# Head quads instead of head pairs in a chunk-selected attention kernel with an MLP behind it

## The chip, the core and the metric

The kernel runs on one core of a Trainium2 chip. The metric is device time in microseconds (us), from the first to the last work of one execution; lower is better. The engines are TensorE (PE; its weight loads are listed apart as PEld), VectorE (DVE), ScalarE (ACT), GpSimd (POOL) and SyncE (SP), which here only issues DMA. Each works through its own instructions in order and waits on semaphores for the others.

## What is computed

Attention over 4 batches and 8 heads of 768 tokens with head dimension 64, each query attending to at most 6 chunks of 32 keys, and a gated MLP on the result. Cut to what matters:

```python
k_min, k_max = k_chunks.min(axis=3), k_chunks.max(axis=3)            # 24 chunks of 32 keys
ub = sum(maximum(q * k_min, q * k_max), axis=-1)                     # bound of each query on each chunk
ub = where(causal, ub, -1e9)
top_chunks = argsort(ub)[..., -6:]
scores = where(chunk of key in top_chunks & (pos_q >= pos_k), q @ k.T / 8, -1e9)
attn = softmax(scores) @ v                                           # x: [4*768, 512]
h = x @ w_in                                                         # 512 -> 2048
out = (h * clip(h + 3, 0, 6) / 6) @ w_out                            # 2048 -> 512, fp32
```

## The kernel before, in words

Heads are worked on in 16 pairs (`i`, four to a batch); the MLP takes half batches of 384 tokens (`g`, 0 to 7). The whole program is a list of short tokens, `ORDER`, written out by hand or by a planner; each token calls one function, and each engine gets its instructions in the order of the list. Nothing is reordered later.

Queries below 192 need no selection, so bounds and masks cover the last 576 (`NQ`). For a pair the tokens are:

- `LK`, `LQ`, `LV` load halves of K, Q and V (pairs 0 to 3), `lk`, `lq`, `lv` whole ones (pairs 4 to 15). For pairs 4 to 15 `load_turned` (L230) reads K and Q in rows of 32 numbers (128 bytes), four DMAs for a pair's K and four for its Q, and `kd`, `qd` (L246, L249) turn them on VectorE in 32x32 blocks; pairs 0 to 3 are turned by TensorE (`KT`, `QT`, L379).
- `kb`, `kp`, `qb` make bf16 copies on ACT or POOL, `mx`, `mn` (L344) reduce K over chunks, `rp` makes relu(q).
- `ud` (L472) computes the bounds of two pairs as f32 matmuls in tiles of 64 rows and 32 columns; `us`, `tr`, `tm`, `se`, `tb` add the causal bias, turn, take the 8 largest of 24, compare with the sixth and turn back, on DVE. `mr` (L499) moves half of the mask rows to the partitions where the mask pass needs them.
- `S.i.u.c` is a unit of scores of a pair in PSUM buffer `c` (a, b or c, two banks each, one head to a bank). There are six units (`UNITS`). The two heads lie in two tiles of 64 rows (L549). For pairs 0 to 9 a second matmul (L554) adds -8192 where a chunk is not chosen. `ex` (L560) takes the exponential on ACT, `af` (L567) the causal triangle on POOL.
- Pairs 10 to 15 (`PRODUCT`) have no mask pass on TensorE. Their masks go to HBM (`sm`, L522: four DMAs a pair), come back spread over 128 partitions (`ml`, L527), are made causal (`am`, L534) and are multiplied onto the exponentials by VectorE (`mu`, L541).
- `A` and `B` (L583) are the products with V for the lower and upper 384 queries, `na`, `nb` the division; `X`/`xe` or the DMA transposes `xt` turn the result for the MLP.

For a half batch, `H.g.f` (L627) is 8 hidden matmuls into one of the buffers a, b, c; `hu` (L635, ACT) and `gt` (L638, DVE) make the gate; `O.g.t.n` (L665) is 4 of the 16 output matmuls of a 128-row tile, in the one-bank buffers x, y as a rule; `ot` (L672) unloads it on ACT and `sa` stores it from the ACT queue (L679). The last tile named by an `st` token is projected and stored in two halves.

At the start, POOL builds the identity (`PRI`), then the bias and mask patterns (`PRP`, L279 to L289, `EG`, L297); DVE clears the buffer `WARM` (`PRD`, L269) and the mask pattern EM (`PRL`, L294); five warm-up matmuls (`Z`, L301) read `WARM`.

SP's loads, mask stores and transposes share eight semaphore lanes: a DMA on a lane waits until the one before it on that lane has landed, and everything behind it on the queue waits too.

Of the kernel before, what the change touches and what calls it, by code (L numbers as in the profile page):

```python
# [9 lines left out]
A = mybir.AluOpType  # L10
# [24 lines left out]
LQ.0.0.0 PRD AQ.0.0.1 AK.0.0.1 LQ.0.1.1 LK.0.0.0 LQ.0.1.0 LK.0.1.0 LK.0.1.1 LQ.2.0.0 LQ.2.0.1 LK.1.0.0 Z.b.5  # L35
AK.1.0.1 PRI QT.0.0.y RP.0.0 PRL RN.0.0 KT.0.0.x LK.2.0.1 AQ.1.0.1 LK.2.0.0 MX.0.0 QT.0.1.b RA.0.1 RP.0.1 QB.0.1
KT.0.1.a PRP EG.3 EG.2 LK.1.1.1 LQ.1.0.0 LK.3.0.0 EG.0 QB.0.0 LQ.2.1.1 LK.1.1.0 MN.0.0 UH.0.0.c QT.2.0.b MN.0.1
MX.0.1 RP.2.0 QB.2.0 KT.1.0.y UB.0.0 LQ.2.1.0 MN.1.0 LQ.1.1.0 KB.0.0 LQ.1.1.1 UH.0.1.c MX.1.0 RN.2.0 LK.3.0.1 KB.0.1
UB.0.1 KT.2.0.x MX.2.0 TH.0.0.a QT.1.0.b QB.1.0 EG.1 KB.1.0 TH.0.1.c MN.2.0 T8.0.0 LQ.3.0.0 LQ.3.0.1 RN.1.0 KB.2.0
KT.1.1.y LK.2.1.1 RP.1.0 QT.2.1.x LK.3.1.0 LK.2.1.0 KB.1.1 T8.0.1 AV.1.0.1 RA.2.1 RP.2.1 QB.2.1 UH.1.0.b SE.0.0  # L40
UH.2.0.a SE.0.1 MN.1.1 UB.1.0 QT.1.1.c RA.1.1 QB.1.1 RP.1.1 TH.1.0.b MX.1.1 LK.3.1.1 UB.2.0 LQ.3.1.0 T8.1.0 QT.3.0.x
RN.3.0 LV.1.0.0 VC.1.0 KT.3.0.y MN.3.0 SE.1.0 TH.2.0.a UH.1.1.c MX.3.0 QB.3.0 UB.1.1 LH.0.0.b LV.0.1.0 AV.0.0.1
MT.0.0 RP.3.0 KT.2.1.x T8.2.0 KB.3.0 LH.0.1.c MT.0.1 SE.2.0 KB.2.1 MX.2.1 TH.1.1.y MN.2.1 S.0.1.b ex.0.1 S.0.0.c
S.0.4.a LQ.3.1.1 ex.0.0 ex.0.4 LV.0.0.0 wl.0 af.0.1 af.0.0 VC.0.0 UH.3.0.b LV.0.1.1 T8.1.1 UB.3.0 LV.2.0.0 KT.3.1.x
MN.3.1 MX.3.1 QT.3.1.c RP.3.1 RA.3.1 QB.3.1 UH.2.1.b SE.1.1 KB.3.1 UB.2.1 S.0.3.a ex.0.3 A.0.y LH.1.0.c MT.1.0
af.0.3 LH.2.0.b MT.2.0 TH.2.1.x LV.1.1.1 S.0.5.c ex.0.5 wc.0 VC.0.1 af.0.5 LV.3.0.1 na.0 LV.1.1.0 S.1.0.b ex.1.0
# [687 lines left out]
```

## Time and profile before

| what | value |
|---|---|
| median of 3 runs | 284.36 us |
| the runs | 282.49, 285.15, 284.36 us |
| span of the profiled execution | 279.9 us |
| its own time beside the span | not on the page; the runs lie 2.6 to 5.2 us above the span |
| PE / PEld / DVE / ACT / POOL busy | 256.5 / 150.8 / 199.9 / 176.8 / 84.8 us |
| DMA packets | 137745, of which 122736 under 512 bytes |
| bytes moved | 46.79 MB; HBM read 36.31, written 8.06 |
| mean granted TensorE clock | 0.985 |

The span runs from the first to the last instruction. Busy time of an engine is the time in which at least one of its instructions is under way; TensorE's matmuls overlap, so a busy PE may still start fewer matmuls than it could. Issuing a DMA is not counted as busy, though it holds the engine that issues it.

### The profile page before, as it was taken

Reading aid. Unit: us, or ns where it says so; the run is one execution under the profiler, and the core shown is the slowest. Engines: PE = TensorE matmul, PEld = TensorE weight load, DVE = VectorE, ACT = ScalarE, POOL = GpSimd, SP = SyncE. Lnnn points to the kernel's source line nnn. Section 1 sums busy time; section 2 is a strip of 40 time slices with the busy share of each in tenths; the row PEclk is TensorE's granted clock in tenths of the full one; section 3 lists DMA queues with packets and bytes.
Section 4 is the critical chain, followed back from the end, with each engine's and each line's share of the span. In section 5 each row is a group of like instructions: output and inputs, shape, how many; then the busy total and the mean of one; then the engine's idle time right before and its main releaser. Section 6 shows DMA issues by size and latency. Waiting matters only on the chain.

```text
span 279.9 us, 6893 instructions
## 1 busy us (share of the span) xinstructions
PE 256.5 (92%) x2639; PEld 150.8 (54%) x2661; DVE 199.9 (71%) x490; ACT 176.8 (63%) x245; POOL 84.8 (30%) x159
## 2 busy tenths in 40 slices
PE   6799998899998999976998976899999999999994
PEld 2467775555445476633545543574455557655543
DVE  3697996997777799939967796575988567735500
ACT  2689994457476899734577659267975678234331
POOL 8216857343315656002006322204222411000000
PEclk9999999999999999997999999799999999999998
DMA  8987897997997899887859869585969641130033
GB/s 165 201 196 207 130 346 122 328 264 190 210 189 165 167 175 171 150 169 135 214 147 227 173 180 193 127 241 86 223 169 291 199 99 38 41 93 0 37 115 112
DMA packets 137745, 46.79 MB, mean 167 GB/s; under 512 B 122736, under 2 KB 128368, under 8 KB 137712
## 3 DMA queue, kind: packets, MB, share of 16 engines
q1 hardware_dynamic: 132000, 39.73, 64.6%
q10 hardware_dynamic: 5712, 6.62, 6.8%
q8 instruction: 21, 0.34, 0.5%
q14 instruction: 12, 0.10, 0.1%
HBM read 36.31 MB, written 8.06 MB: 158 GB/s over the span
## 4 chain that ended last, share of the span: by engine, by line
PE 61%; DMA 10%; SPq 8%; issue 6%; DVE 5%; POOL 4%; ACT 4%; ACTq 0%; DVEq 0%; POOLq 0%
PE PBb L627 8%; PE PSy L665 8%; PE PBa L627 8%; PE PBc L627 8%; PE PSx L665 7%; SPq L230 6%; DMA QS<-in_q_dram 3%; DMA out_dram<-OT 3%; PE PSx L583 3%; PE PBa L665 2%; PE PBb L665 2%; POOL PT L567 2%; PE PSy L583 2%; SPq L522 2%; ACT PT L560 2%
## 5 line engine op out<-in xcount | busy, mean ns | idle before, releaser
L627 PEld LDWEIGHTS <-WIN 128*128 128x128 bf16 x512 | 49.5, 99 | 35.3 <-issue 1.8
L665 PEld LDWEIGHTS <-GT 128*128 128x128 bf16 x368 | 34.6, 99 | 40.6 <-issue 3.7
L560 ACT ACTIVATE PT<-PBa 128x1024 bf16<-128x1024 f32 (+2 forms) x33 | 30.9, 937 | 16.1 <-PE PBa L549 11.4
L665 PE MATMUL PSy<-WOUT,GT 128*128 128x512 bf16 x149 | 38.3, 385 | 1.1 <-issue 0.7
L567 POOL TENSOR_SCALAR_AFFINE_SELECT PT<-PT 128x256 bf16<-128x256 bf16 x72 | 30.5, 444 | 24.5 <-ACT PT L560 18.3
L627 PE MATMUL PBb<-XT,WIN 128*128 128x384 bf16 x176 | 33.4, 335 | 1.1 <-POOL WIN L262 1.1
L635 ACT ACTIVATE U<-PBb 128x768 bf16<-128x768 f32 x22 | 17.9, 813 | 20.9 <-PE PBb L627 20.9
L560 ACT ACTIVATE PT<-PBb 128x1024 bf16<-128x1024 f32 (+2 forms) x32 | 29.1, 909 | 3.2 <-PE PBb L554 2.2
L665 PE MATMUL PSx<-WOUT,GT 128*128 128x512 bf16 x119 | 30.1, 382 | 0.7 <-issue 0.3
L627 PE MATMUL PBa<-XT,WIN 128*128 128x384 bf16 x168 | 30.7, 326 | 0.0
L627 PE MATMUL PBc<-XT,WIN 128*128 128x384 bf16 x168 | 30.7, 326 | 0.0
L583 PEld LDWEIGHTS <-PT 128*128 128x128 bf16 x672 | 24.1, 98 | 11.7 <-POOL PT L567 4.5
L560 ACT ACTIVATE PT<-PBc 128x1024 bf16<-128x1024 f32 (+2 forms) x31 | 28.7, 927 | 2.2 <-PE PBc L549 1.6
L635 ACT ACTIVATE U<-PBc 128x768 bf16<-128x768 f32 x21 | 17.0, 811 | 19.3 <-PE PBc L627 19.3
L638 DVE SCALAR_TENSOR_TENSOR GT<-U,PBc 128x768 bf16<-128x768 bf16 x21 | 19.9, 947 | 10.4 <-ACT U L635 10.4
L638 DVE SCALAR_TENSOR_TENSOR GT<-U,PBb 128x768 bf16<-128x768 bf16 x22 | 20.8, 946 | 6.5 <-ACT U L635 6.5
L549 PEld LDWEIGHTS <-KB 64*128 64x128 bf16 x320 | 15.6, 94 | 18.0 <-issue 11.9
L541 DVE TENSOR_TENSOR PT<-PT,WS 128x256 bf16<-128x256 bf16 (+2 forms) x42 | 17.1, 440 | 7.5 <-POOL PT L567 3.4
L344 DVE TENSOR_REDUCE KM<-KSM 128x24 f32<-128x768 f32 x24 | 22.2, 944 | 0.3
L635 ACT ACTIVATE U<-PBa 128x768 bf16<-128x768 f32 x21 | 17.0, 812 | 7.7 <-PE PBa L627 7.6
L534 POOL TENSOR_SCALAR_AFFINE_SELECT WS<-WS 128x256 bf16<-128x256 bf16 x18 | 7.6, 425 | 46.8 <-DMA WS<-SCR 46.8
L638 DVE SCALAR_TENSOR_TENSOR GT<-U,PBa 128x768 bf16<-128x768 bf16 x21 | 19.9, 946 | 2.3 <-ACT U L635 2.2
(187 smaller groups left out, 417.5 us busy)
## 6 DMA issues: line engine op xcount, KB each, us to landing
QS<-in_q_dram SPq DMA_DIRECT2D x62, 96.0 KB, 2.9
KSM<-in_k_dram SPq DMA_DIRECT2D x62, 96.0 KB, 3.3
out_dram<-OT ACTq DMA_DIRECT2D x23, 256.0 KB, 2.6
VS<-in_v_dram SPq DMA_DIRECT2D x12, 384.0 KB, 4.5
WS<-in_moe_w_in_dram SPq DMA_DIRECT2D x4, 1024.0 KB, 5.9
WS<-in_moe_w_out_dram SPq DMA_DIRECT2D x4, 1024.0 KB, 7.0
SCR<-MTM SPq DMA_DIRECT2D x24, 72.0 KB, 2.7
WS<-SCR SPq DMA_DIRECT2D x6, 288.0 KB, 4.0
```

What stands on the lines that cost most here:

```text
L230: nc.sync.dma_start(dst[g:g + CH].rearrange("p (n d) -> p n d", d=CH), x[b, 2 * hp + e].rearrange("(n t) d -> t n d", t=CH)[:, :, CH * d:C ...
L344: nc.vector.tensor_reduce(out=KM[i % 4][:, m, 0:NCH], in_=k_turned(i).rearrange("p (c w) -> p c w", w=CH), axis=AX.X, op=(A.max, A.min)[m] ...
L534: nc.gpsimd.affine_select(out=T, in_=T, pattern=[[0, 2], [1, P]], compare_op=A.is_ge, fill=0.0, base=0, channel_multiplier=-1)
L541: nc.vector.tensor_tensor(out=T, in0=T, in1=mask_view(i, j, lo, q0 + n), op=A.mult)
L549: nc.tensor.matmul(PSB[c][:, e, at:at + n], lhsT=K[rows, j * P:(j + 1) * P], rhs=Q[rows, q0:q0 + n], start=True, stop=q0 + n <= Q0 or i in ...
L560: nc.scalar.activation(PT[i % 3][u][:, :, 0:n], PSB[slot["S", i, u]][:, :, 0:n], ACT.Exp, scale=float(scale))
L567: nc.gpsimd.affine_select(out=T[:, :, lo:lo + P], in_=T[:, :, lo:lo + P], pattern=[[0, 2], [1, P]], compare_op=A.is_ge, fill=0.0, base=0, ...
L583: nc.tensor.matmul(O[:, e, t, :], lhsT=PT[i % 3][u][:, e, lo:lo + P], rhs=VB[i % 4][:, j, e, :], start=(j == 0), stop=(j == qb))
L627: nc.tensor.matmul(PSB[c][:, ff, 0:GRP], lhsT=WIN[:, kt, (2 * f + ff) * P:(2 * f + ff + 1) * P], rhs=XT[g % 3][:, kt, :], start=(kt == 0), ...
L635: nc.scalar.activation(slot["R", g, f][:], PSB[slot["H", g, f]][:, :, 0:GRP], ACT.Relu, bias=3.0)
L638: nc.vector.scalar_tensor_tensor(out=GT[g % 2][:, 2 * f:2 * f + 2, :], in0=slot["R", g, f][:], scalar=6.0, in1=PSB[slot["H", g, f]][:, :, ...
L665: nc.tensor.matmul(PSS[c], lhsT=GT[g % 2][:, f, t * P:(t + 1) * P], rhs=WOUT[:, f, :], start=(f == 0), stop=(f == FT - 1))
```

## The change

Pairs 4 to 15 become six quads `n` = 2 to 7 of four heads, one head to each 32 partitions, with the 64 numbers of a head as two halves `x` of 32 along the free axis. Pairs 0 to 3 keep their functions.

- `lk`, `lq` load a quad's K or Q with four DMAs whose rows are 256 bytes. K and Q of the pairs 0 to 3 and of the quads share one buffer `STAGE`; a quad's K or Q takes one of three thirds of it, in turn.
- `kd`, `qd`, `kb`, `qb`, `mx`, `mn`, `rp` work on halves of a quad; all K copies are now on ACT.
- `ud` computes a quad's bounds in tiles of 32 rows and 32 columns, 64 matmuls; `us`, `tr`, `tm`, `se`, `tb` come in two halves each.
- `mv` gathers the mask rows of one head with four POOL copies of 32x144.
- `SQ.n.u.c.cc` is a unit of scores of four heads in tiles of 32 rows, in two of the three PSUM buffers: two passes for the two halves `x`, and a mask pass for every quad. The way of pairs 10 to 15 over HBM goes, with `sm`, `ml`, `am` and `mu`, and `mr` and `kp` with it; `af` treats all of their units.
- The exponentials of the quads rotate over four sets of buffers; the fourth lies in the weight staging buffer.
- The loads and the output stores that went through ACT's queue move to SP (`sa` becomes `st`); the tile projected in halves is now (7, 1), one before the last.
- `ORDER` is new throughout. `PRP` stands ahead of `PRI`, and `PRI` and `PRL` ahead of `PRD`; the first load is K.

```diff
 ORDER = """
-LQ.0.0.0 PRD AQ.0.0.1 AK.0.0.1 LQ.0.1.1 LK.0.0.0 LQ.0.1.0 LK.0.1.0 LK.0.1.1 LQ.2.0.0 LQ.2.0.1 LK.1.0.0 Z.b.5
-AK.1.0.1 PRI QT.0.0.y RP.0.0 PRL RN.0.0 KT.0.0.x LK.2.0.1 AQ.1.0.1 LK.2.0.0 MX.0.0 QT.0.1.b RA.0.1 RP.0.1 QB.0.1
+LK.0.0.1 PRP PRI PRL EG.2 EG.1 PRD Z.y.5 PRA EG.0 EG.3 LK.0.1.1 LK.0.0.0 KT.0.0.y LQ.0.0.0 MX.0.0 MN.0.0 LQ.0.0.1
+QT.0.0.b QB.0.0 LQ.0.1.1 LK.0.1.0 RN.0.0 RP.0.0 KT.0.1.a MX.0.1 KB.0.0 MN.0.1 LQ.0.1.0 QT.0.1.x KB.0.1 LK.1.1.1
...
+A.3.x na.3 VC.1.1 S.3.4.b ex.3.4 S.2.4.a mx.2.0 X.0.1.c B.1.0.x xe.0.1 af.3.5 kx.2 B.1.1.x ex.2.4 nb.0 H.0.1.b
...
+SQ.4.0.c.a ex.8.0 O.3.0.2.y O.3.0.3.y af.11.1 vc.11 SQ.4.5.b.c ot.2.2 ex.8.5 af.8.5 af.8.0 ex.9.5 af.9.5 ex.9.0
...
+    STAGE = const.tile([P, 6, S], FP32, name="STAGE")
...
+    def staged(m, n):
+        at = (1 + 2 * (n - FIRST_QUAD) + "kq".index(m)) % 3
+        return STAGE[:, 2 * at:2 * at + 2].rearrange("p h (n x t) -> p h n x t", x=2, t=CH)
...
+    PT.append([spare[w][:, at:at + 2 * n].rearrange("p (e n) -> p e n", e=2) for (w, at), n in zip(SPARE, COLS)])
+
+    def pt(i, u):
+        return PT[i % 3 if i < NPAIR else i % 4][u]
...
-    def load_turned(dst, x, i):
-        b, hp = divmod(i, NPAIR)
-        for e in range(2):
-            for d in range(2):
-                g = D * e + CH * d
-                nc.sync.dma_start(dst[g:g + CH].rearrange("p (n d) -> p n d", d=CH),
-                                  x[b, 2 * hp + e].rearrange("(n t) d -> t n d", t=CH)[:, :, CH * d:CH * (d + 1)])
+    def load_rows(m, x):
+        def issue(n, *only):
+            b, first = divmod(4 * n, H)
+            dst = staged(m, n).rearrange("p h n x t -> p (h n) (x t)")
+            for g in only or range(4):
+                nc.sync.dma_start(dst[CH * g:CH * (g + 1)], x[b, first + g].rearrange("(n t) d -> t n d", t=CH))
+        return issue
+
+    def turn(m):
+        def issue(n, h):
+            T = staged(m, n)[:, h].rearrange("p n x t -> p (n x t)")
+            nc.vector.transpose(out=T, in_=T)
+        return issue
...
+    def chunk_bounds(w):
+        def issue(n, h):
+            dst = KM4[n % 2][:, w, :, NCH // 2 * h:NCH // 2 * (h + 1)].rearrange("p x n -> p n x")
+            nc.vector.tensor_reduce(out=dst, in_=staged("k", n)[:, h], axis=AX.X, op=(A.max, A.min)[w])
+        return issue
...
+    def bounds(n, c, cc):
+        slot["U", n] = c, cc
+        raw = staged("q", n).rearrange("p h n x t -> p (h n) x t")[:, TOPK:]
+        pos = RPA[:].rearrange("p x (n t) -> p n x t", t=CH)
+        for w, R in enumerate((pos, raw)):
+            for x in range(2):
+                for part in range(4):
+                    for g in range(4):
+                        rows = slice(CH * g, CH * (g + 1))
+                        nc.tensor.matmul(PSB[(c, cc)[g // 2]][CH * part:CH * (part + 1), g % 2, 0:NQ // 4],
+                                         lhsT=KM4[n % 2][rows, w, x, :], rhs=R[rows, :, x, 8 * part:8 * part + 8],
+                                         start=(w == 0 and x == 0), stop=(w == 1 and x == 1),
+                                         tile_position=(CH * g, CH * part))
...
+    def gather_rows(n, g):
+        for part in range(4):
+            w = NQ // 4
+            nc.gpsimd.tensor_copy(MQ[n % 2][CH * g:CH * (g + 1), w * part:w * (part + 1)],
+                                  MT4[n % 2][CH * part:CH * (part + 1), w * g:w * (g + 1)])
...
-    def mask_apply(i, u):
-        for at, j, q0, n in UNITS[u]:
-            lo = max(q0, Q0)
-            T = PT[i % 3][u][:, :, at + lo - q0:at + n]
-            nc.vector.tensor_tensor(out=T, in0=T, in1=mask_view(i, j, lo, q0 + n), op=A.mult)
...
+    def scores_quad(n, u, *both):
+        slot["S", 2 * n, u], slot["S", 2 * n + 1, u] = both
+        K, Q = KB4[n % 2], QB4[n % 2]
+        chosen = MQ[n % 2][:].rearrange("p (r n t) -> p n r t", r=4, t=8)
+        for at, j, q0, w in UNITS[u]:
+            lo = max(q0, Q0)
+            for x in range(2):
+                for g in range(4):
+                    rows = slice(CH * g, CH * (g + 1))
+                    nc.tensor.matmul(PSB[both[g // 2]][:, g % 2, at:at + w], lhsT=K[rows, x, j * P:(j + 1) * P],
+                                     rhs=Q[rows, x, q0:q0 + w], start=(x == 0), stop=False, tile_position=(CH * g, 0))
+            for g in range(4):
+                rows = slice(CH * g, CH * (g + 1))
+                nc.tensor.matmul(PSB[both[g // 2]][:, g % 2, at + lo - q0:at + w], lhsT=EM[rows, j, g % 2, :],
+                                 rhs=chosen[rows, (lo - Q0) // CH:(q0 + w - Q0) // CH], start=False, stop=True,
+                                 tile_position=(CH * g, 0))
```

More of the change, by code (lines that the diff above doesn't have):

```diff
@@ L233, in load_k @@
[L233 to L249 removed]
+    E0 = XT[2][:].rearrange("p a b -> p (a b)")[0:CH, 0:S].rearrange("p (a b) -> p a b", b=P)
@@ new lines, in bias_add, with turn_bounds, bounds_rows, top8 @@
+    def bias_add(n, p):
+        nc.vector.tensor_tensor(out=UB4[:, 2 * p:2 * p + 2], in0=PSB[slot["U", n][p]][:, :, 0:NQ // 4],
+                                in1=BIAS4[:].unsqueeze(1).to_broadcast([P, 2, NQ // 4]), op=A.add)
+    def turn_bounds(n, p):
+        nc.vector.transpose(out=UBT[:, HQ * p:HQ * (p + 1)], in_=UBM[:, HQ * p:HQ * (p + 1)])
+    def bounds_rows(p):
+        return UBT[:, HQ * p:HQ * (p + 1)].rearrange("p (s c) -> p s c", c=CH)
+    def top8(n, p):
+        for s in range(9):
+            nc.vector.max(out=T8D[:, 9 * p + s, :], in_=bounds_rows(p)[:, s, :])
```

383 lines of the change are left out of this document (139 added, 244 removed).

## The prediction

> **What bounds the kernel now.** I read the page first, then the chain of waits, then a table of windows cut where each half batch's first hidden matmul starts (39.9, 56.6, 107.4 us and so on).
>
> ```profile
> span 279.9 us, 6893 instructions
> PE 61%; DMA 10%; SPq 8%; issue 6%; DVE 5%; POOL 4%; ACT 4%; ACTq 0%; DVEq 0%; POOLq 0%
> ```
>
> TensorE (PE) holds 61% of the chain; DMA and the queue that issues it (SPq) hold 18%. The windows give span, then PE, weight loads, DVE, ACT and POOL busy, the clock, the DMA share and GB/s:
>
> ```profile
> 0.00:39.90 39.90, 35.04 (x567) 24.42 (x568) 30.49 (x123) 30.45 (x52) 20.98 (x44) 1.00 0.87 206
> 39.90:56.60 16.70, 14.18 (x166) 9.02 (x164) 14.04 (x28) 8.58 (x12) 10.32 (x18) 1.00 0.94 226
> 56.60:107.40 50.80, 48.96 (x534) 28.10 (x537) 41.43 (x104) 36.94 (x50) 21.47 (x34) 1.00 0.92 197
> 107.40:132.20 24.80, 20.90 (x195) 11.86 (x196) 19.90 (x35) 14.59 (x20) 5.96 (x10) 0.93 0.80 147
> 132.20:176.90 44.70, 38.87 (x394) 21.82 (x398) 35.13 (x83) 29.99 (x40) 12.89 (x28) 0.99 0.84 192
> 176.90:199.90 23.00, 22.79 (x216) 12.53 (x216) 15.34 (x42) 15.01 (x20) 3.85 (x7) 0.95 0.62 152
> 199.90:232.60 32.70, 32.44 (x287) 17.93 (x291) 23.65 (x52) 23.08 (x30) 8.58 (x19) 1.00 0.73 191
> 232.60:250.00 17.40, 17.35 (x153) 10.41 (x151) 12.29 (x22) 8.02 (x11) 0.78 (x2) 1.00 0.21 56
> 250.00:279.90 29.90, 26.02 (x151) 14.76 (x151) 7.63 (x8) 10.12 (x15) 0.00 (x0) 0.97 0.17 62
> ```
>
> I call these stages S (start) and H0 to H7. In H4 to H6 PE is never idle for more than 0.3 us. It is idle 4.9 us in S, 2.5 in H0, 1.8 in H1, 3.9 in H2, 5.8 in H3 and 3.9 in H7. Up to H3 the DMA engines are 80 to 94% busy. The chain shows why PE waits, and what its units cost:
>
> ```profile
> 51.29 1.30 PE PBc L627 x8
> 75.84 0.86 PE PBb L665 x4
> 111.45 0.46 PE PSy L583 x15
> ...
> 134.96 3.70 DMA out_dram<-OT
> 138.73 0.69 SPq L522
> ...
> 144.08 3.41 DMA WS<-SCR
> ```
>
> One `H` is 1.30 us of PE, one `O` 0.86, one `B` (15 matmuls) 0.46, so one `A` (12) 0.37. At 135 us the SP queue stands 3.7 us behind an output store, issues eight mask stores of 0.6 us each, and waits 3.4 us for the masks to come back: the HBM round trip of pairs 10 to 15 is on the path.
>
> **The change, part by part.**
>
> *The mask detour goes.* Its 36 `mask_load`, 24 stores and 36 `mask_apply` go. Rows for what leaves or is new, by line:
>
> ```profile
> L541 DVE TENSOR_TENSOR PT<-PT,WS 128x256 bf16<-128x256 bf16 (+2 forms) x42 | 17.1, 440 | 7.5 <-POOL PT L567 3.4 <-ACT PT L560 2.9 <-POOL WS L534 0.9
> L541 DVE TENSOR_TENSOR PT<-PT,MX 128x384 bf16<-128x384 bf16 (+2 forms) x18 | 7.1, 424 | 1.2 <-ACT PT L560 1.1
> L499 POOL COPY MS<-MTM 64x288 bf16<-64x288 bf16 x6 | 2.5, 422 | 0.4
> L297 POOL COPY EM<-MX 32x768 bf16<-32x768 bf16 x4 | 3.3, 818 | 0.2
> L337 POOL CAST KB<-KSM 128x768 bf16<-128x768 f32 x6 | 4.9, 824 | 0.1
> L560 ACT ACTIVATE PT<-PBa 128x1024 bf16<-128x1024 f32 x24 | 24.8, 1032 | 12.1 <-PE PBa L549 9.4 <-PE PBa L554 1.8 <-DVE GT L638 0.6
> QS<-in_q_dram SPq DMA_DIRECT2D x62, 96.0 KB, 2.9
> 117.23 0.34 ACTq L679 DMA_DIRECT2D out_dram<-OT  x1
> ```
>
> DVE loses 60 multiplies, 42 x 0.440 + 18 x 0.424 = 26 us, most of it in H3 to H5.
>
> *Row loads.* A quad's K or Q becomes four DMAs of 256-byte rows instead of eight of 128-byte rows. Over six quads that is 48 issues for 96, with half the packets. Their landing lies between the 2.9 us of the 96 KB row and twice that; the order leaves several hidden units between load and turn, so I cost it at nothing. Without that cover the late one is `kd` or `qd`, then `ud`.
>
> *Stores to SP.* ACT loses 23 issues of 0.34 us (8 us), SP gains them. A store waits for `ot`, and the next K, Q or V loads queue behind it, and `kd`, `qd` or a V cast behind those. SP, some 80 issues shorter, has room, and the order puts each store a few instructions after its `ot`: nothing. Without that room each of the 23 would hold the loads as at 135 us, up to 3.7 us, and only the few loads that are late already would pass it on. The six K casts of L337 move to ACT (5 us there by their 0.82), so ACT is 3 us lighter in all.
>
> *Masks gathered on POOL.* Each `mv` is four copies of 32x144, 96 copies in all. The two copy rows put one between 0.1 and 0.42 us; a line through them gives 0.30, which I take: 29 us of POOL, four `mv` = 4.8 us ahead of a quad's first scores. The cover is the hidden units the order puts there (in H1 ten, 13 us); without it PE waits up to 4.8 us a quad, 29 us in all. Behind an `mv` on POOL wait the causal passes `af` and V casts, and for them the `A` and `B` of the pair; POOL is 21 of 51 us busy in H1 and 13 of 45 in H3, so I let them through at no cost. POOL's rest (18 more `af`; no `am`, `kp`, `mr`) is nearly even.
>
> *Scores in 32-row tiles.* Before, two 64-row tiles run together:
>
> ```profile
> 95.51 1.02 PE L665 MATMUL PSx<-WOUT,GT 128*128 128x512 bf16 x4
> 96.47 0.34 PE L549 MATMUL PBb<-QB,KB 64*128 64x384 bf16 x2
> ...
> 97.75 0.72 PE L472 MATMUL PBa<-RP,KM 64*32 64x288 f32 x16 [0.35 <-DVE KM L349]
> 98.23 0.72 PE L472 MATMUL PBa<-QS,KM 64*32 64x288 f32 x16
> 99.29 0.34 PE L549 MATMUL PBb<-QB,KB 64*128 64x384 bf16 x2 [0.33 <-ACT PT L560]
> 99.45 0.20 PE L554 MATMUL PBb<-MTM,EM 64*128 64x96 bf16 x1
> ```
>
> Two 384-column matmuls are followed by the next 0.16 us later: one pass at 2.4 columns a ns. L472 runs eight tiles together (16 matmuls, two instructions each per product, in 0.48 us). If four 32-row tiles run together, a quad streams 2 x 2688 columns for both d halves and 2432 for the masks, 3.25 us, so 0.54 a `SQ` unit. Pairs 4 to 9 needed the same per quad twice over for the mask (4.3 us), pairs 10 to 15 had no mask pass (2.2 us): with three quads of each kind, nothing changes. `ud` has twice the passes at half the width, the same columns, in 128 instructions for 32. If the 0.48 us of L472 is not its columns but 16 starts of 30 ns, an `ud` grows by 96 x 0.03 = 2.9 us, 17 us in six quads; 0.48 us is exactly 2 x 288 columns at two cycles each, so I take the low end, nothing. The same holds for the 12 weight loads a segment in a `SQ`. If only two tiles run together, the price is 19.5 us more; a gain I exclude, as the columns are the same. I take four, after L472, which keeps two row groups and four column groups going.
>
> A sentence beside this: the Trainium skill, "TensorE: Matmul & The Clock Gate", Part 3, measured four 32-row tiles at 3.07 times one, not 4. By that the 19.5 us of streaming would be 25.4, and the total about 6 us longer. No run so far shows such tiles.
>
> *Mode changes.* Four `O` matmuls from 95.51 end streaming at 96.375 (4 x 0.216, from the 0.86); the scores start at 96.47. So 0.095 us goes at each change of tile shape. Counted along the two orders these are 96 before, 125 after: +2.8 us.
>
> *The new order at the start.*
>
> ```profile
> 1.08 0.29 POOL masks.py:199 TENSOR_SCALAR_AFFINE_SELECT IDENT<-IDENT 128x128 f32<-128x128 f32 x1
> 1.29 2.32 PE L301 MATMUL PBb<-MX 128*128 128x512 bf16 x5 [1.29 <-DVE MX L269]
> 1.31 0.33 POOL L279 MEMSET BIASM<- 64x288 f32 x1
> 1.72 1.35 POOL L284 TENSOR_SCALAR_AFFINE_SELECT BIASM<-BIASM 32x96 f32<-32x96 f32 x4
> 1.90 0.70 DVE L294 MEMSET EM<- 128x768 uint32 x1
> 3.12 0.73 POOL L286 MEMSET MX<- 32x768 bf16 x1
> 3.80 0.87 PE L379 MATMUL PSy<-IDENT,QS 128*128 128x128 f32 x3 [0.19 <-DMA QS<-in_q_dram]
> 4.71 0.33 ACT L401 ACTIVATE RP<-PSy 128x192 f32<-128x192 f32 x1 [0.99 <-PE PSy L379]
> 4.83 0.85 POOL L289 TENSOR_SCALAR_AFFINE_SELECT MX<-MX 32x768 bf16<-32x768 bf16 x1
> ```
>
> Now `PRP` (1.31 to 5.68: 4.4 us) stands ahead of `PRI` on POOL, and `PRL` ahead of `PRD` on DVE. So the identity is ready at 0.8 + 4.4 + 0.5 = 5.7 us; DVE copies it, clears EM (0.70) and only then WARM: 7.1; the five warm-up matmuls (2.3) hold PE to 9.4; the first transpose (0.87) ends at 10.3 though its data land near 5; ACT, behind a second transpose, starts at 10.8 instead of 4.71. Before `H.0.1` ACT then has 34.2 us of work (23 exponentials, by the 1.03 for 1024 columns and in proportion, 21.2; 28 casts and Relus of 0.33 to 0.5, 13.0), because the bank it needs is freed by the exponential before the last (before, 30.45 us were done). 10.8 + 34.2 and 1.4 of waiting: S = 46.4, 6.5 more.
>
> *The later stages.* After S I add PE's units and 0.095 a mode change. H3, as an example, holds 8 `H`, 16 `O`, 4 `A`, 4 `B`, 11 `SQ`, an `ud` (1.0) and 24 changes: 10.4 + 13.8 + 1.5 + 1.8 + 6.0 + 1.0 + 2.3 = 36.8, where before had 38.9 busy and 5.8 idle. In the same way: H0 12.7, H1 48.3, H2 21.3, H4 24.8, H5 32.7, H6 16.4. The same sum for before gives H5 32.3 and H6 17.4, where the windows have 32.7 and 17.4. Slack: H0 +1.3 (weights arrive one by one), H1 +2.0 (DVE and ACT nearly as full), H2 +1.5, H3 +1.4. H7 stays 29.9: its units are the same, and it ends, as now, with the store of a whole tile. What H0 to H3 lose are waits: for V behind K issues (H0), for K and Q (H2), for the masks (H3). Where a gone wait exposes the next one, that is DVE, which the multiplies leave free in H3 but not in H1 and H2. Sum: 46.4 + 14.0 + 50.3 + 22.8 + 38.2 + 24.8 + 32.7 + 16.4 + 29.9 = 275.5. The page has no time of its own beyond the span; the median 284.36 lies 4.4 above it (the runs 2.6 to 5.2). Forecast 280.0 us: S gives back 6.5, H0 to H3 give 11.7.
>
> **The rivals.**
>
> *Tiles two at a time.* L549 shows two row tiles and nothing more. Place: the 36 `SQ` from H1 to H5. Price 19.5 us, of which some 4 hide where ACT is the fuller engine. It decides as soon as a 384-column pass of four takes over 0.24 us. 296, slower. For it: no 32-row tile in the trace. Against: eight tiles in L472.
>
> *The bank pair.* A `SQ` takes two of three two-bank buffers, so the next one stands on PE until an exponential (1.03) of the last has freed one, with the `O` queued behind it. Against: ACT is not the fullest engine and `O` units lie between. It decides from 0.3 us a unit: 36 x 0.3 = 11 us, 291, slower.
>
> *The waits only move.* S costs its 6.5, and H1 and H2 stay at 50.8 and 24.8 since DVE is 41 of 51 and 20 of 25 us busy there anyway: +2.5 on the forecast, and 1.7 more if PE's clock drops as in H2 before (0.93 of 24.8 us). 284, the same. For it: DVE's share; against: PE's 3.9 us idle in H2 are more than its clock explains.
>
> *Every stage at PE's sum.* S takes 42 because K, Q and V have all landed when work starts, and no stage has slack (6.2 less): about 269. For it: H4 to H6 run so already. Against: the stages from S to H3 never did.
>
> **How the numbers follow.** Forecast 0.34, every stage at PE's sum 0.12, waits only move 0.17, tiles 0.15, bank pair 0.22. A measurement of this kernel can tell about 1% from no change. Faster by over 1%: 0.46; within 1%: 0.17; slower: 0.37. The likeliest case alone spans 275 to 283. The range reaches from under the best rival, 268, to the tiles' 296; a gather without cover (309) is left out.
>
> **What would show it.** Right: first ACT work near 10.8 and first hidden matmul near 46; no SP wait for stores ahead of loads over 2 us; a quad's 384-column pass in 0.16 us; H3 under 39. Wrong: `SQ` units over 0.8 us of PE, PE idle before L489 for an exponential, POOL copies over 0.4 us, or H1 beyond 52.

## The result and the profile after

The changed kernel takes 284.78 us (median of 20 runs, 282.80 to 286.44) against 282.61 us for the kernel before in the same comparison (20 runs, 280.83 to 285.15). The ratio is 1.0083, 95% interval 1.0057 to 1.0110: it is slower by 0.8%, where 280.0 us, faster by 1.5%, was forecast. Below, a run's median is over all its executions, while its ratio leaves out those that lie more than 1.5% above its fastest. The first and fourth part of the page of after show the same picture from both ends, a span 2.3 us longer and a chain in which TensorE holds a little more than before:

```profile
span 282.2 us, 8568 instructions
...
PE 63%; POOL 9%; DMA 8%; DVE 5%; issue 4%; ACT 3%; SPq 1%; POOLq 0%; DVEq 0%; ACTq 0%
```

The SP queue has left the chain (8% to 1%), so the mask detour is gone; POOL has come into it (4% to 9%). The windows of after, cut at the first hidden matmul of each half batch, have the columns of the prediction's table:

```profile
0.00:46.80 46.80, 34.68 (x562) 24.84 (x563) 32.32 (x121) 32.12 (x54) 21.85 (x47) 1.00 0.69 175
46.80:62.50 15.70, 13.72 (x257) 9.17 (x254) 11.42 (x20) 7.16 (x10) 8.59 (x16) 1.00 0.97 241
62.50:115.80 53.30, 51.15 (x789) 27.92 (x787) 47.88 (x123) 39.33 (x53) 29.08 (x64) 1.00 0.93 199
115.80:137.90 22.10, 22.10 (x316) 13.11 (x309) 21.23 (x41) 14.66 (x20) 5.38 (x17) 1.00 0.67 122
137.90:176.00 38.10, 38.09 (x582) 20.88 (x581) 24.75 (x65) 28.60 (x38) 17.13 (x42) 1.00 0.51 108
176.00:202.00 26.00, 26.00 (x398) 14.85 (x398) 15.51 (x40) 21.25 (x29) 8.63 (x25) 1.00 0.50 104
202.00:235.10 33.10, 33.10 (x425) 19.26 (x422) 13.91 (x26) 20.64 (x27) 13.90 (x37) 1.00 0.13 38
235.10:251.50 16.40, 16.40 (x93) 8.97 (x92) 8.36 (x11) 7.35 (x10) 0.00 (x0) 1.00 0.25 73
251.50:282.20 30.70, 26.33 (x153) 14.69 (x151) 7.55 (x8) 10.12 (x15) 0.00 (x0) 0.99 0.14 52
```

Before these can be compared, one cut of the prediction has to be put right. Its 56.6 us is not the first hidden unit of half batch 1 in the kernel before but the third: the order runs `H.1.5`, `H.1.6`, `H.1.1` before it goes back to `H.0.6`. The first one starts at 54.0, and the windows of before with that cut are

```profile
39.90:54.00 14.10, 11.58 (x151) 7.46 (x148) 11.51 (x19) 7.77 (x11) 9.13 (x17) 1.00 0.89 218
54.00:107.40 53.40, 51.56 (x556) 29.66 (x554) 43.96 (x112) 37.75 (x51) 22.66 (x35) 1.00 0.93 200
```

The forecast's own lengths for H0 and H1 were counted from `H.1.5`, so they stand beside these:

| stage | before | forecast | after | after less forecast |
|---|---|---|---|---|
| S | 39.9 | 46.4 | 46.8 | +0.4 |
| H0 | 14.1 | 14.0 | 15.7 | +1.7 |
| H1 | 53.4 | 50.3 | 53.3 | +3.0 |
| H2 | 24.8 | 22.8 | 22.1 | -0.7 |
| H3 | 44.7 | 38.2 | 38.1 | -0.1 |
| H4 | 23.0 | 24.8 | 26.0 | +1.2 |
| H5 | 32.7 | 32.7 | 33.1 | +0.4 |
| H6 | 17.4 | 16.4 | 16.4 | 0 |
| H7 | 29.9 | 29.9 | 30.7 | +0.8 |
| span | 279.9 | 275.5 | 282.2 | +6.7 |

From H2 to H6 TensorE is busy for 100% of the windows and the forecast holds within 1.2 us a stage. The 6.7 us are lost in H0 and H1 for the most part: 4.7 of them. The start came as forecast, row by row in the timeline:

```profile
5.37 0.29 POOL masks.py:199 TENSOR_SCALAR_AFFINE_SELECT IDENT<-IDENT 128x128 f32<-128x128 f32 x1
5.70 0.23 DVE L274 CAST IDENTB<-IDENT 128x128 bf16<-128x128 f32 x1 [5.70 <-POOL IDENT masks.py:199]
6.77 0.27 DVE L250 MEMSET XT<- 128x256 uint32 x1
7.10 2.32 PE L282 MATMUL PSy<-XT 128*128 128x512 bf16 x5 [7.10 <-DVE XT L250]
...
10.74 0.48 ACT L387 CAST QBA<-PBb 128x384 bf16<-128x384 f32 x1 [3.74 <-PE PBb L379]
```

Where H0 goes wrong is told by the chain of waits there, and by the largest entry of TensorE's waits in H0 and H1:

```profile
43.47 0.45 POOL VB L373
...
44.37 6.97 DMA VS<-in_v_dram
...
51.47 0.51 POOL VB L373
51.97 1.84 POOL WIN L243
...
53.83 0.37 SPq L239
...
54.24 8.23 DMA WS<-in_moe_w_in_dram
...
62.53 1.89 POOL WIN L243
```

```profile
PE PBb L566 <- POOL WIN L243: 1.3, 1, 1.3
```

A V cast on POOL (43.47) frees a V buffer, a V load goes out at 44.37 and needs 6.97 us beside a weight load and a Q load, its cast is done at 52.0, and only then the weight cast `wc.2`, which stands behind it on POOL, makes the weights that `H.0.4` waits 1.3 us for and frees the buffer for the next weight load (53.83). The DMA share is 0.97 in H0, while between 30 and 40 us, just before, it was 0.2 to 0.4. In the kernel before POOL made `wc.2` first and found V there for `VC.3.1`:

```profile
43.16 1.89 POOL L262 CAST WIN<-WS 128x2048 bf16<-128x2048 f32 x1
...
46.07 0.51 POOL L373 CAST VB<-VS 128x384 bf16<-128x384 f32 x1
```

Three things the prediction could not see in the trace of before are seen now. One score unit of four heads in the timeline (two lines for the two PSUM buffers, the second left out):

```profile
147.37 1.04 PE L604 MATMUL PSy<-WOUT,GT 128*128 128x512 bf16 x4
148.34 0.34 PE L489 MATMUL PBc<-QBA,KBA 32*128 32x384 bf16 x2
...
148.51 0.33 PE L489 MATMUL PBc<-QBA,KBA 32*128 32x384 bf16 x2
...
148.67 0.33 PE L493 MATMUL PBc<-MQ,EM 32*128 32x384 bf16 x2
...
149.10 0.50 PE L566 MATMUL PBa<-XT,WIN 128*128 128x384 bf16 x2
```

Four 384-column matmuls in 32-row tiles start every 0.165 us: four at a time, as forecast. A quad's bounds, first and last row of the 128 instructions and what follows, and below them the same product of before:

```profile
196.14 0.31 PE L323 MATMUL PBb<-RPA,KMA 32*32 32x144 f32 x2
...
197.85 0.30 PE L323 MATMUL PBc<-STAGE,KMA 32*32 32x144 f32 x2
198.08 0.61 PE L604 MATMUL PSx<-WOUT,GT 128*128 128x512 bf16 x2
```

```profile
195.13 0.72 PE L472 MATMUL PBc<-RP,KM 64*32 64x288 f32 x16
195.64 0.69 PE L472 MATMUL PBc<-QS,KM 64*32 64x288 f32 x16
196.26 0.39 PE L549 MATMUL PBa<-QB,KB 64*128 64x384 bf16 x4
```

They take 1.94 us of TensorE instead of 1.13, though the columns are the same. And the gather is as dear as forecast:

```profile
L353 POOL COPY MQ<-MTM 32x144 bf16<-32x144 bf16 x96 | 29.4, 306 | 29.3 <-DVE MTM L347 25.0
```

### The profile page after: what moved, and what is told of

Read it like the earlier page. It is cut to its first block, busy times and chain, and to the rows that moved or that the text cites. A ratio compares the mean times of both kernels' runs of the same rounds, so it can differ in the third digit from the quotient of the medians.

```text
span 282.2 us, 8568 instructions
## 1 busy us (share of the span) xinstructions
PE 261.6 (93%) x3549; PEld 153.7 (54%) x3549; DVE 182.9 (65%) x448; ACT 181.2 (64%) x251; POOL 104.6 (37%) x246
## 4 chain that ended last, share of the span: by engine, by line
PE 63%; POOL 9%; DMA 8%; DVE 5%; issue 4%; ACT 3%; SPq 1%; POOLq 0%; DVEq 0%; ACTq 0%
PE PSx L604 12%; PE PSy L604 9%; PE PBa L566 8%; PE PBc L566 7%; PE PBb L566 7%; POOL MQ L353 4%; DMA WS<-in_moe_w_in_dram 3%; PE PSy L522 3%; DMA VS<-in_v_dram 2%; DMA STAGE<-in_q_dram 2%; PE PBb L604 2%; POOL WIN L243 2%; PE PBc L489 2%; PE PBb L489 2%; PE PBa L489 2%
## 5 line engine op out<-in xcount | busy, mean ns | idle before, releaser
L604 PEld LDWEIGHTS <-GT 128*128 128x128 bf16 x368 | 32.9, 98 | 38.9 <-issue 3.5
L604 PE MATMUL PSx<-WOUT,GT 128*128 128x512 bf16 x176 | 43.4, 380 | 0.6 <-POOL WOUT L243 0.6
L353 POOL COPY MQ<-MTM 32x144 bf16<-32x144 bf16 x96 | 29.4, 306 | 29.3 <-DVE MTM L347 25.0
L604 PE MATMUL PSy<-WOUT,GT 128*128 128x512 bf16 x144 | 35.1, 380 | 0.0
L574 ACT ACTIVATE U<-PBa 128x768 bf16<-128x768 f32 x23 | 18.7, 812 | 22.9 <-PE PBa L566 22.1
L566 PE MATMUL PBb<-XT,WIN 128*128 128x384 bf16 x160 | 29.3, 326 | 1.7 <-POOL WIN L243 1.3
L566 PE MATMUL PBc<-XT,WIN 128*128 128x384 bf16 x168 | 30.8, 326 | 0.0
L229 DVE STREAM_TRANSPOSE STAGE<-STAGE 128x768 f32<-128x768 f32 x24 | 23.0, 965 | 6.3 <-DMA STAGE<-in_q_dram 3.6
L499 ACT ACTIVATE PT<-PBb 128x1024 bf16<-128x1024 f32 (+2 forms) x25 | 23.5, 940 | 3.6 <-PE PBc L493 1.8
L499 ACT ACTIVATE PT<-PBa 128x1024 bf16<-128x1024 f32 (+2 forms) x24 | 22.7, 948 | 2.9 <-PE PBa L493 2.7
L301 DVE TENSOR_REDUCE KMA<-STAGE 128x24 f32<-128x768 f32 x24 | 22.1, 940 | 0.1
L522 PEld LDWEIGHTS <-PT 128*128 128x128 bf16 x546 | 19.1, 97 | 3.9 <-issue 1.3
L489 PEld LDWEIGHTS <-KBA 32*128 32x128 bf16 x480 | 9.3, 92 | 16.5 <-issue 13.8
```

What stands on the lines that cost most here:

```text
L229: nc.vector.transpose(out=T, in_=T)
L301: nc.vector.tensor_reduce(out=dst, in_=staged("k", n)[:, h], axis=AX.X, op=(A.max, A.min)[w])
L353: nc.gpsimd.tensor_copy(MQ[n % 2][CH * g:CH * (g + 1), w * part:w * (part + 1)], MT4[n % 2][CH * part:CH * (part + 1), w * g:w * (g + 1)])
L489: nc.tensor.matmul(PSB[both[g // 2]][:, g % 2, at:at + w], lhsT=K[rows, x, j * P:(j + 1) * P], rhs=Q[rows, x, q0:q0 + w], start=(x == 0), ...
L499: nc.scalar.activation(pt(i, u)[:, :, 0:n], PSB[slot["S", i, u]][:, :, 0:n], ACT.Exp, scale=float(scale))
L522: nc.tensor.matmul(O[:, e, t, :], lhsT=pt(i, u)[:, e, lo:lo + P], rhs=VB[i % 4][:, j, e, :], start=(j == 0), stop=(j == qb))
```

## The experiments

The theory after the first comparison: the forecast's mechanisms are right, and what it missed is the chain of V and weights in H0 and H1, with the bounds as a second term. The rivals: the late start reaches further than S; VectorE or POOL's gather fills H1; the stores hold up the loads. All runs are compared by medians (the changed kernel's is 284.78) and by the spans and stages of their profiles (282.2).

How far such comparisons reach can be read from the runs. They were measured in six further groups on five chips, and the kernel before, run again beside each group, had medians from 282.52 to 285.57 us. The changed kernel itself was measured in the first comparison only. The run that differs from it just in the queue of its stores has a ratio of 1.0026 (0.9984 to 1.0068). So the 0.8% belong to the first comparison; that the change is not 1.5% faster shows in both. A difference of about 1 us between medians of different groups decides nothing here, and a stage of one profile can differ by some tenths of a us (H3 38.1 in the changed kernel, 38.4 in that run).

**The prologue as before.**

```diff
-LK.0.0.1 PRP PRI PRL EG.2 EG.1 PRD Z.y.5 PRA EG.0 EG.3
+LK.0.0.1 PRD PRI PRL PRP EG.2 EG.1 Z.y.5 PRA EG.0 EG.3
```

> The changed kernel with the prologue in the order of before: PRD ahead of PRI and PRL, and PRP behind them. Theory (the late start is passed on whole): warm-up matmuls from about 1.3 us instead of 7.1, first ACT work near 5 instead of 10.7, first hidden unit near 41 instead of 46.8, median 278 to 281, some 5 under the changed kernel. Rival (the transfers of H0 set the pace, since the DMA engines have share 1.01 there): the first hidden unit comes earlier but the first unit of half batch 1 stays near 60 to 62, H0 gets longer by what S gets shorter, median 283 or more.

Measured: 281.26 us, ratio to before 0.9914 (0.9871 to 0.9957), span 279.3.

```profile
6.43 0.48 ACT L387 CAST QBA<-PBb 128x384 bf16<-128x384 f32 x1 [4.12 <-PE PBb L379]
```

```profile
0.00:44.60 44.60, 37.28 (x562) 25.52 (x563) 32.33 (x121) 32.33 (x54) 21.89 (x47) 1.00 0.77 186
44.60:59.40 14.80, 13.57 (x257) 9.10 (x254) 11.53 (x20) 7.16 (x10) 8.57 (x16) 1.00 1.02 245
```

ACT starts 4.3 us earlier, but the first hidden unit comes only 2.2 us earlier (44.6, not 41). Behind its first work ACT is busy for 30.8 us of the 38.2 that are left of S, where it was 30.6 of 36.1: two of the 4.3 us have turned into waits of ACT. So the prologue's order is worth 2.9 us of span (3.5 by the medians). The rival's stall in H0 did not come, H0 is 0.9 us shorter.

**The weight cast ahead of the V cast.**

```diff
-af.3.3 VC.3.1 B.3.0.y wc.2 H.0.4.b
+af.3.3 wc.2 VC.3.1 B.3.0.y H.0.4.b
```

> The changed kernel with the weight cast wc.2 ahead of the V cast VC.3.1 on POOL. Theory (H0 waits because that cast stands behind a late V load): the idle 1.31 us of PE ahead of H.0.4 goes, the first unit of half batch 1 starts 1.0 to 1.4 us earlier than 62.55, median 283.4 to 284. Rival (the next weight or V transfer is late anyway, the DMA engines being full): the wait reappears at another unit of H0 and the median stays within 0.4 us of the changed kernel's 284.8.

Measured: 283.82 us, ratio 0.9989 (0.9947 to 1.0031), span 280.4; H0 15.1, H1 51.8. The wait of 1.3 us ahead of `H.0.4` is gone; H0 gains only 0.6, but the later weight loads move up too and H1 gains 1.5. That profile is the fastest of the ten executions, and by the medians the whole gain is 1.0 us. So this run supports the chain without deciding it, and the place of the gain was not as expected.

**Half of the bounds' instructions, and half of their columns.**

```diff
-        for w, R in enumerate((pos, raw)):
+        for w, R in enumerate((pos,)):
...
-  start=(w == 0 and x == 0), stop=(w == 1 and x == 1),
+  start=(w == 0 and x == 0), stop=(x == 1),
```

> The changed kernel without the second product of the bounds (raw q with the minimum), which is left out: 64 instructions a quad instead of 128. Theory (bounds cost 1.94 us of TensorE a quad, twice their 0.96 of columns, and TensorE is the bound wherever they stand): each takes 0.97 us, six of them 5.8 us less, median 279 to 280. Rival (they lie in the shadow of DVE and ACT work, as the prediction's zero would have it): median 283 to 285.

```diff
-  PSB[...][CH * part:CH * (part + 1), g % 2, 0:NQ // 4], ... rhs=R[rows, :, x, 8 * part:8 * part + 8]
+  PSB[...][CH * part:CH * (part + 1), g % 2, 0:NQ // 8], ... rhs=R[rows, :, x, 8 * part:8 * part + 4]
```

> The changed kernel with every bounds matmul over 72 query columns instead of 144 (half of the queries' bounds are left out), the number of instructions the same. Theory (128 starts of 15 ns each, whatever the columns): a quad's bounds still take 1.9 us, median within 0.8 us of the changed kernel's 284.8. Rival (the time goes with the columns, 16 small tiles not running all together): 0.97 us a quad, and the median as without the second product, 279 to 280.

Measured: 283.26 us, ratio 1.0013 (0.9964 to 1.0061), span 280.9 without the second product; 283.30 us, ratio 0.9986 (0.9943 to 1.0029) with the narrow one, whose profile (span 284.5) had a clock of 0.981 as a whole but 1.00 in the stretch shown. A quad's bounds take 1.05 and 1.46 us:

```profile
198.94 0.25 PE L323 MATMUL PBb<-RPA,KMA 32*32 32x72 f32 x2
...
200.23 0.24 PE L323 MATMUL PBc<-STAGE,KMA 32*32 32x72 f32 x2
200.40 0.82 PE L604 MATMUL PSx<-WOUT,GT 128*128 128x512 bf16 x3
```

Neither account of the 1.94 us holds alone: with half the columns it falls by a quarter. And taking 0.89 us off each of six quads moved the span by 1.3 us, not 5.3. By stages H2 and H4 got 0.9 us shorter each (21.2, 25.1), just what was taken off their one quad; H0 (15.9), H1 (52.8) and H3 (38.5) hardly moved. My theory that the bounds count wherever they stand fell: in these two profiles they count in H2 and H4 alone.

**V and the first weights earlier.** POOL stands idle for 8 us before 31 us, at a causal pass that waits for its exponential, with the V casts queued behind it.

```diff
+LV.0.1.1 LV.0.0.1 LV.0.1.0 LV.0.0.0 LV.1.0.1 LV.1.0.0 LV.1.1.1 wl.0 LV.1.1.0 wl.1     (behind lk.2)
+VC.0.0 VC.1.0 VC.0.1 VC.1.1 LV.3.0.0 LV.3.0.1 LV.2.0.0 LV.2.0.1 LV.3.1.0 LV.3.1.1     (ahead of af.0.3)
+wc.0 wl.2     (behind af.2.0; all of these tokens go from their old places)
```

> The changed kernel with the loads and casts of V for pairs 0 to 3 and of the first two weight pieces moved ahead: POOL casts V (VC.0.0, VC.1.0, VC.0.1, VC.1.1) in the 8 us in which it waits for an exponential before 31 us, the V loads that wait for these casts follow at once, and wl.1 stands behind wl.0. Theory (H0 and H1 lie at the chain V load, V cast, weight cast, next weight load, while the DMA engines stand at 0.2 to 0.4 of their time from 30 to 40 us): the V loads issued at 37 to 44 us go out at 29 to 35, H0 and H1 together take 65 to 67 us instead of 69.05, median 281 to 283. Rival (H1 is full by itself, DVE 45 of 51 us): H0 and H1 together stay above 68, median 284 to 285.

Measured: 281.31 us, ratio 0.9924 (0.9889 to 0.9958), span 278.6.

```profile
0.00:46.60 46.60, 33.64 (x562) 24.05 (x563) 32.27 (x122) 32.15 (x54) 22.28 (x48) 1.00 0.85 204
46.60:60.10 13.50, 13.35 (x256) 9.02 (x254) 11.03 (x19) 7.15 (x10) 9.65 (x16) 1.00 0.84 209
60.10:112.00 51.90, 49.97 (x782) 27.98 (x789) 47.08 (x123) 39.51 (x53) 27.61 (x64) 1.00 0.86 197
```

H0 and H1 together take 65.4 us instead of 69.0, and nothing else moves: all 3.6 us of span come from there. By the medians it is 3.5 us, and 3.6 against the run with the stores on ACT's queue, which was measured beside it. This edit alone turns the slower kernel into a faster one.

**The late prologue in the kernel before.**

```diff
-LQ.0.0.0 PRD AQ.0.0.1
+LQ.0.0.0 PRP PRI PRL PRD AQ.0.0.1     (PRP, PRI, PRL go from their old places)
```

> The kernel before with the changed kernel's prologue order (PRP, PRI, PRL ahead of PRD). Theory, after the prologue run (which gave back 2.9 us of span, not 6.5): the late start costs the kernel before 2 to 4 us, ratio 1.007 to 1.015, since its loads were not all there earlier. Rival (the prediction's step, the whole delay of ACT's first work of some 6 us is passed on): ratio 1.018 to 1.025.

Measured: 287.04 us, ratio 1.0124 (1.0060 to 1.0187): +3.5 us. ACT's first work comes at 10.08 instead of 4.71, 5.4 us later, and the first hidden unit at 45.0 instead of 39.95, 5.1 us later: S takes over nearly all of the delay, and the later stages win some of it back. By its ratio this order alone costs the kernel before about as much as the whole change did, the intervals overlapping. The rival that all of the 6 us is passed on to the end (1.018 and more) lies at the very end of the interval.

**Stores on ACT's queue again.** All `st` tokens but `st.7.1` become `sa`.

> The changed kernel with 23 of the 24 output stores issued from ACT again. Theory (stores on SP cost nothing, as predicted): within 1 us of the changed kernel's 284.8, the loads of K, Q and V behind them being early enough; ACT's 8 us of issue are hidden too, because TensorE is the bound from H2 on. Rival (SP's waits for unloaded tiles, 81 us in nine places, hold the loads behind them): H2 to H5 get shorter, 2 us or more under 284.8. Other rival (ACT is the bound): 2 us or more above.

Measured: 284.94 us, ratio 1.0026 (0.9984 to 1.0068), span 282.1; H2 22.1, H3 38.4, H4 26.0. The stores' queue does not matter, although SP spends about half of its waiting in the changed kernel on them:

```profile
SPq L615 <- ACT OT L611: 81.3, 9, 21.5
```

**Both edits.** The prologue and the early V and weights together.

> The changed kernel with both edits, the old prologue order and the early V and weights. Theory (two separate causes): their gains add, median 278 to 280.5, ratio 0.975 to 0.988 to the kernel before. Rival (both gains are the same wait, seen from two ends): no better than the better one of the two alone, median 281 or more.

Measured: 279.16 us, ratio 0.9839 (0.9790 to 0.9888), span 277.0: faster than both kernels. Most of the gains add (2.9 and 3.6 us of span alone, 5.2 together). In S the clock of this profile is 0.96, where it was 1.00 in the two alone, but that does not explain the rest: two of the four executions ran at 1.00, with spans of 277.3 and 277.4. H0 and H1 take 13.5 and 51.3 us, together 64.8, where the forecast had 64.3.

```profile
PE 84%; DMA 5%; DVE 2%; issue 2%; ACT 2%; POOL 2%; SPq 1%; DVEq 0%; POOLq 0%
```

TensorE's share of the chain goes from 63% to 84%, POOL's from 9% to 2%.

**Two load queues.** Both edits, and

```diff
-LQ.0.0.0 ... LQ.0.0.1 ... LQ.0.1.1 ... LQ.0.1.0 ... LQ.1.1.0 ... LQ.1.1.1
+AQ.0.0.0 AQ.0.0.1 AQ.0.1.1 AQ.0.1.0 AQ.1.1.0 AQ.1.1.1     (ahead of PRD)
```

> The kernel with both edits (old prologue order, early V and weights), and six of the first Q loads issued from ACT's queue, as the kernel before issued eight loads there. Theory (what is left of the longer start is the one queue: in the changed kernel SP issues a 96 KB load every 0.53 us, 185 GB/s, which is what the windows from 5 to 25 us move): the K loads go out 3 us earlier, the first hidden unit starts at 43 to 44.5 instead of 45.7, median 277 to 278.5. Rival (the chain of TensorE, ACT and VectorE sets S whatever the loads): first hidden unit within 0.6 us of 45.7, median 279.

Measured: 278.39 us, ratio 0.9775 (0.9709 to 0.9842), span 277.4; S 44.5, H1 52.9. S is 1.2 us shorter than with both edits, whose profile had a clock of 0.96 there, and H1 1.6 us longer. The intervals overlap; whether the one queue costs S anything is left open.

**Half of the bounds' instructions on top of both edits.**

> The kernel with both edits, and the second product of the bounds left out. Alone that took 0.89 us of TensorE off each quad's bounds, 5.4 in six, but only 1.3 us off the span. Theory (H0 and H1 were bound by the V and weight chain, so there the longer bounds were hidden; with the chain shorter TensorE is the bound): H0 and H1 together get 1.5 to 2.7 us shorter than the 64.75 of both edits, the span 3 to 4.5 us shorter than 277.0. Rival (VectorE, 45 of 51 us busy in H1, hides them as before): H0 and H1 within 0.8 us of 64.75, the span at most 2 us shorter.

Measured: 279.92 us, span 277.5; H0 12.6, H1 53.9. H0 gains 0.9 us, H1 loses 2.6, the largest wait of TensorE being

```profile
PE PBc L492 <- POOL MQ L352: 1.9, 1, 1.9
```

So theory and rival were both wrong: what TensorE no longer does in H1 it spends on waits, for the gather above all (1.0 us for a gate and 0.8 us for relu(q) come next).

**The gather twice, and a quarter of it.**

```diff
-        for part in range(4):
+        for part in (0, 1, 2, 3) * 2:
```

> The changed kernel with each of the 96 gather copies done twice, which puts 29.4 us more work on POOL. Theory (the gather has cover, as predicted; TensorE waits 0.3 us for it in all): under 6 us slower than the changed kernel, at most 1 us a quad. Rival (the cover is just used up by the single copies): 15 to 29 us slower, TensorE waiting up to 4.9 us a quad ahead of the mask pass.

Measured: 324.14 us, ratio 1.1405 (1.1314 to 1.1497), 39 us slower, beyond even the rival's 29. TensorE's waits of that run:

```profile
PE PBc L493 <- POOL MQ L353: 12.8, 4, 6.0
PE PBb L493 <- POOL MQ L353: 8.4, 2, 5.8
...
PE PBa L493 <- POOL MQ L353: 3.9, 2, 2.6
PE PSy L522 <- POOL PT L506: 2.7, 1, 2.7
```

25 us are waits for the gather, of the 29 us that it adds, and 2.7 are for a causal pass behind it. The granted clock is 0.947 in this run where it is 1.00 in the changed kernel's, which is where I would look for the rest, but no run separates it.

```diff
-        for part in range(4):
+        for part in range(1):
```

> The changed kernel with only the first of the four gather copies of each head (three quarters of the mask rows are left out, the buffers cleared once): 22 us less on POOL. With double copies the kernel was 40 us slower, so there is no spare cover; this tells whether the single copies are already short of it. Theory (covered, but only just; TensorE waits 0.3 us for them in all, and H1 is bound by the V and weight chain): within 1.5 us of the changed kernel's 284.8. Rival (the chain of VectorE's selection and POOL's copies sets H1, and H1 shrinks by most of two quads' 8 us): 3 us or more faster, H1 under 51.

Measured: 284.39 us, ratio 0.9998 (0.9956 to 1.0040), span 282.9, H1 53.2: no gain that the profile shows. The single copies are covered, with little to spare: of the doubled run's 29 us more, 25 came back as waits, so at most some 4 found cover.

**One search for the eight largest instead of nine**, on top of both edits.

```diff
-        for s in range(9):
+        for s in range(1):
```

> The kernel with both edits, and only one of the nine searches for the eight largest done in each half of a quad's selection (the other eight are left out, T8D is cleared once): 96 VectorE instructions of some 0.1 us go, 32 of them in H1. Theory (with the V and weight chain shortened, H1 stands at VectorE, 46.8 of its 51.2 us busy): H1 goes from 51.2 to 49 or less, the span from 277.0 to 275 or less. Rival (H1 is now at TensorE's sum with its own small waits, as the prediction had it at 50.3): H1 stays within 0.7 us of 51.2.

Measured: 280.47 us, ratio 0.9940 (0.9889 to 0.9991), span 279.0.

```profile
61.80:112.60 50.80, 49.78 (x781) 27.70 (x787) 42.30 (x75) 39.35 (x53) 27.53 (x63) 1.00 0.84 199
```

```profile
POOL VB L373 <- DMA VS<-in_v_dram: 4.0, 1, 4.0
```

VectorE has 4.6 us less in H1, and H1 is 0.5 us shorter: it is at TensorE's own sum, not at VectorE. S was 48.2 in this run, where it was 45.7 with both edits: POOL stood 4.0 us at the V cast `VC.1.1`, 1.5 there, with causal passes behind it, a weakness of my early placement.

**That V cast two causal passes later**, on top of two load queues.

```diff
-VC.0.0 VC.1.0 VC.0.1 VC.1.1 LV.3.0.0 LV.3.0.1 LV.2.0.0 LV.2.0.1 LV.3.1.0 LV.3.1.1 ... af.2.0
+VC.0.0 VC.1.0 VC.0.1 LV.3.0.0 LV.3.0.1 LV.2.0.0 LV.2.0.1 ... af.2.0 VC.1.1 LV.3.1.0 LV.3.1.1
```

> The kernel with both edits and two load queues, and the V cast VC.1.1 (with the two V loads behind it) moved two causal passes back, since in the run with one maximum POOL stood 4.0 us at that cast with causal passes queued behind it, and TensorE 2.8 us behind those. Theory (that stall is what makes S vary from run to run): first hidden unit at 43.5 to 44.5, H0 and H1 as with both edits, median 277 to 278.5, spread under 3 us. Rival (the V loads are then late for H0 again): H0 and H1 grow by 1 us or more, median 279 or more.

Measured: 278.35 us (276.38 to 280.39), ratio 0.9799 (0.9745 to 0.9853), span 275.6; S 44.2, H0 13.5, H1 51.4. The profiled span is the shortest of all profiles, but the executions vary by 4.0 us, where under 3 was expected, and it cannot be told from two load queues without it.

## Why the prediction was wrong, step by step

**The start: right in size, wrong in its make-up.** ACT started at 10.74 (10.8 forecast) and S took 46.8 (46.4). But ACT's work behind that start was 30.6 us (32.12 less the table load and one dummy exponential), not 34.2, and its waits 5.4, not 1.4: two errors that cancelled, so the total was right by luck. The prediction added up durations, and ACT's instructions overlap: the exponential of 1.02 us at 30.84 is followed by the next at 31.74. The 6.9 us that S lost are 6.0 of start and 1.5 of work, less 0.6 of waits. Of the 6.0, 4.3 are the prologue's order. The other 1.7 (ACT's first work is at 6.43 with the old prologue, 4.71 before) go with K ahead of Q: Q's first transpose starts at 5.52 there, at 3.80 before. No run separates that. And a start given back is not all kept: undoing the prologue brought 2.9 us of span, since ACT then waits 2 us more.

**The step that failed: the slack of H0 and H1.** The prediction named the mechanism ("weights arrive one by one") and gave it 1.3 us in H0, and 2.0 in H1 for full engines. Measured against its own sums of TensorE work (12.7 and 48.3) the slack was 3.0 and 5.0. The 1.3 and 2.0 were chosen, not read. The kernel before, by the same sums of its units (11.3 and 50.2), had 2.8 and 3.2 there. The prediction let H0 win its wait for V behind K issues. V's load no longer stands behind them, but V stayed late: the load in the chain above took 6.97 us (2.90 for the one that H0 waited for before), POOL stood 4.0 us for it at `VC.3.1`, and the chain of V load, V cast, weight cast and weight load became longer: `wc.2` stood ahead of `VC.3.1` before, at 43.16, and stands behind it now, at 51.97. The bounds' longer run (0.8 us a quad, one in H0 and two in H1) is part of the slack too, but with 0.89 us a quad taken off, H0 and H1 together stayed at 68.7 for 69.0. The wrong cut at 56.6 hid how little H0 had to give: it seemed to hold 16.7 us of which 2.7 could go. The early V and weights gave back 3.6 of the 4.7 us, and with both edits H0 and H1 came out at 64.8 against 64.3. The prediction's own sign of being wrong, H1 beyond 52, came with 53.3.

**The bounds: taken at the wrong end.** The prediction bounded 0 to 2.9 us a quad and took 0. It was 0.8 (1.94 for 1.13), 4.9 in all, of which by the half-bounds run some 1.6, the quads of H2 and H4, lay on the path: it is most of H4's 1.2. The Trainium skill, "TensorE: Matmul & The Clock Gate", Part 3, has sixteen 32x32 tiles with 512 columns at 10.6 times one, not 16, which the prediction did not use: as an estimate 11.3 ns an instruction instead of 7.5, 0.5 us more a quad. The trace agrees in the sign and has more, 13.6 ns.

**The gather: price right, cover wrong.** 0.306 us a copy (0.30 forecast), 29.4 us in all (29). TensorE waits 0.3 us for it in the changed kernel. But the cover was said to be ten hidden units, 13 us; the doubled copies came back as waits for the most part, while quartering them gained nothing, so the order had used nearly all of the cover.

**What held.** Four tiles at a time; about 0.1 us at a mode change (`L604` streams 0.86 us from 147.37, the scores start at 148.34); stores free on SP, though the sign named against it, an SP wait of over 2 us for a store, did come (21.5 us at the longest); row loads nearly hidden (192 KB land in 5.2 to 5.3 us, within 2.9 to 5.8, and VectorE waits 6.4 us for them in all); and the mask detour's end worth what was said, H3 38.1 for 38.2. The Trainium skill, "TensorE: Matmul & The Clock Gate", Part 3, has four 32-row tiles with 512 columns at 3.07 times one; the trace does not agree for a steady stream of them, four 384-column passes in 0.165 us being 9.3 columns a ns against 2.4 for one, 3.9 times.

**The time around the span.** 4.4 us were added, since the median of three lay so far above the profiled span. In the 20 runs of the changed kernel each time lies 1.7 to 1.9 us above its own span; the profiled execution of before was one of the shorter ones. With 1.8 us in its place the forecast would have been 277.3 and missed by 7.5 us instead of 4.8.

**The rivals.** The waits-only-move rival came nearest in time (284), and H1 did stay (53.4, 53.3), but by luck: it gave H2 no gain, where H2 went from 24.8 to 22.1, and its reason was VectorE, where H1 moved by 0.5 with 4.6 us of VectorE work taken away (on top of both edits). The bank pair did not show: TensorE waits 0.8 us ahead of scores (`L489`) in the whole changed kernel, none of it for an exponential. H7's 0.8 was not tested.

## What to carry to other kernels

Where a stage has slack now, ask which wait makes it and whether the change removes that wait; if not, keep the slack of before in the sum instead of a smaller one (here 67.0 us for H0 and H1, of the 69.0 measured, instead of 64.3). Cut stages at the same unit in both kernels before subtracting. A load is late because of what its issue waits for: when the transfers are idle just ahead of a stage in which they are full, look at the in-order queue (here a causal pass on POOL) that holds the cast that holds the buffer.

## What the runs showed of the hardware

Small matmuls in 32x32 tiles do not cost their columns alone. The 128 f32 instructions of a quad's bounds start 13.6 ns apart at 144 columns and 10.3 ns apart at 72 (1.73 and 1.31 us from the first to the last start), where sixteen tiles at full rate would need 7.5 and 3.75 (an estimate from the kernel before, whose eight tiles took 0.48 us for 2 x 288 columns): some 6 ns for each instruction beside its columns. Four 32-row tiles with 384 columns show no such loss, a pass of four every 0.165 us. And work on an engine with 37% load, the gather on POOL, cost more than its own length when doubled: 39 us for 29.4, in a run whose clock was 0.947 instead of 1.00.
